# Other places for the accumulating loads of two batches, and six early groups, in an attention and MoE kernel

## The chip, the core and the metric

The kernel runs on one core of a Trainium2 chip. The metric is device time in microseconds (us) of one launch; lower is better. Before the change it is 992.26 us, the median of three runs (989.83 to 993.4).

A core has five engines, each with its own instruction queue worked in order. TensorE (PE in the profile) multiplies matrices into PSUM banks. ScalarE (ACT) evaluates functions such as exp. VectorE (DVE) does elementwise work. GpSimd (POOL) and SyncE (SP) serve here mainly to issue DMA transfers. Engines wait for each other through semaphores.

## The reference

Batches: 4. Each has 12288 queries of 128 channels and a key-value map of 384 x 32 positions.

```
kv_pool = kv.reshape(B, H//4, 4, W//4, 4, C).mean(axis=(2, 4))    # 768 pooled rows per batch
k = v = kv_pool.reshape(B, -1, C) @ w_sr
s = q @ k.transpose(0, 2, 1) / sqrt(C)
x = softmax(s) @ v                                                # 49152 tokens x 128
h = x @ w_in                                                      # 128 -> 2048
out = (h * sigmoid(1.702 * h)) @ w_out                            # 2048 -> 128
```

## The kernel before

**Tiles.** A group is 512 tokens; there are 96, 24 to a batch. In attention a group has 6 chunks (128 pooled rows each), in the MoE part 16 (128 of the 2048 hidden channels each). A chunk is filled by one 512-column matmul on TensorE (L358 in attention, L600 in MoE), and ScalarE evaluates three chunks at a time from PSUM into `ag` (L360 exp, L602 GELU). Chunks are drained by further matmuls: L371 multiplies by `v`, L610 by `w_out`. VectorE then normalises attention output into `x` (L394, L397) or turns MoE output for the store (L621).

**Stages.** `BOUNDS` makes three rounds: groups 0 to 23, 24 to 71, and 72 to 95. Each round does the attention of its groups and then their MoE. So batch 0 is used in the first attention, batches 1 and 2 in the second, and batch 3 in the third.

**The order of work is planned in Python** when the program is built: a loop over `seq` (fills) and `todo` (drains) keeps model clocks `now`, `dve` and `end` with costs such as `FIXED` and `CHUNK`, and decides what comes next on TensorE and VectorE. On the chip each engine simply works through its list.

**ScalarE is relieved by VectorE.** The first groups of rounds 2 and 3 are *early*: `EARLY = (2, 4)` of them have their exp computed by VectorE (a polynomial, `early_exp`, L439 to L452) during the MoE stage before. They need slots at the bottom of `ag`, which `LOW` keeps clear from a given MoE group on. `rolling` lists attention chunks, and `lent` MoE chunks, that VectorE does within their own stage.

**Keys of batches 1 to 3.** The pooling sum over four by four positions is done partly by DMA. `add_kv(b, n)` issues two loads, one for each half, of the n-th of eight slices; from the second slice on they add to what lies in `kvs` (L174, GpSimd's queue). Such a load waits for the landing of the one before it on the same half. `use_kv(b, a)` then puts a sum of the two halves on VectorE (`sum_kv`, L180) and queues three short jobs for the planner: a transpose on TensorE (L185), the keys (L193) and the values (L200). The first of these sums needs all 16 loads of its batch.

**What is issued when** stands in tables, keyed by the group whose first fill comes up: `ADD_KV` and `USE_KV` for the above; `CAST` and `CAST_MOE` for the casts of q to bfloat16 in DRAM (L210, GpSimd); `TURN` and `TURN_MOE` for the transposing loads of q (L216, SyncE); `W_IN` and `W_OUT` for the attention groups at which the MoE weights are loaded (L561, L564, GpSimd). GpSimd's transfers are timed by `gate()`: a tiny memset on VectorE at that point of its list (L529), and one on GpSimd that waits for it (L530).

```
if i == W_IN:
    gate()
    nc.gpsimd.dma_start(out=w_in_sb, in_=moe_w_in)
```

**Attention output** leaves SBUF and comes back transposed: after every six groups SyncE stores a part to DRAM (`put_away`, L512) and reads it back with a DMA transpose (`bring_back`, L517). Output stores (L623) are on SyncE too.

Of the kernel before, what the change touches and what calls it, by code (L numbers as in the profile page):

```python
# [24 lines left out]
def kernel(  # L25
# [8 lines left out]
    JC = J // 128  # L34
    d_ff = moe_w_in.shape[1]
    FCH = d_ff // 128
# [9 lines left out]
    TS = 3  # L46
# [12 lines left out]
    BOUNDS = (0, GB, 3 * GB, NG)  # L59
    R = len(BOUNDS) - 1  # L60
    XS = NS // 2
    EARLY = (2, 4)
    AG = 102

    cpool = ctx.enter_context(tc.tile_pool(name="const", bufs=1))
# [42 lines left out]
    now = 0.0  # L108
# [60 lines left out]
    def add_kv(b, n):  # L169
        i, w = divmod(n, r)  # L170
        if n == 0:
            kv_sums[b] = kvsum.tile([Hp, 2, Wp, C], F32, name="kvs")
        for i2 in range(2):
            nc.gpsimd.dma_start(out=kv_sums[b][:, i2], in_=kv_p[b, i, w, :, i2],  # L174
                                **({"accum_op": ADD} if n else {}))
# [32 lines left out]
    def cast_q(s):  # L208
        sl = slice(s * SG, (s + 1) * SG)
        nc.gpsimd.dma_start(out=q_bf[sl, :].rearrange("(p i) c -> p (i c)", p=128),  # L210
                            in_=q_flat[sl, :].rearrange("(p i) c -> p (i c)", p=128))

    def load_qT(s):
        qTs[s] = qpool.tile([128, 1, SG], BF, name="qT")
        nc.vector.memset(qTs[s][:, 0, 0:1], 0.0)
        nc.sync.dma_start_transpose(out=qTs[s], in_=q_bf[s * SG:(s + 1) * SG, :])  # L216
# [116 lines left out]

    ahead = [range(b, b + n) for b, n in zip(BOUNDS[1:], EARLY)]
    early = [i for part in ahead for i in part]
    rolling = [(i, JC - 1) for i in (*range(35, 70, 6), 84)]
    lent = [(g, FCH - 1) for g in (*range(28, 37, 4), 74, 77, 79, 82, 84, 87, 89, 92, 94)]
    borrowed = []
    for n in range(R):
        borrowed += [("a",) + c for c in rolling if round_of(c[0]) == n]  # L340
# [148 lines left out]
    steps, early_todo = None, []  # L489
# [35 lines left out]
    def gate():  # L525

        one = gate_tile[:, gates[0] % 8:gates[0] % 8 + 1]
        gates[0] += 1
        nc.vector.memset(one, 0.0)  # L529
        nc.gpsimd.memset(one, 0.0)  # L530

    TURN = {6: 3, 7: 4, 8: 5, 76: 22, 80: 23}
    TURN.update({i: i // 4 + 3 for i in range(BOUNDS[1] + 4, 61, 4)})
    TURN[26] = 9
    TURN_MOE = {3: 6, 21: 7, 22: 8, 68: 19, 69: 20, 70: 21}
    CAST = {0: [5], 14: [6]}
    CAST_MOE = {1: 7, 2: 8, 3: 9, 4: 10, 5: 11, 6: 12, 16: 13, 17: 14, 18: 15, 19: 16, 20: 17, 21: 18,
                46: 19, 47: 20, 48: 21, 49: 22, 50: 23}
    ADD_KV = {("a", i): (1, i - 15) for i in range(15, 23)}
    ADD_KV.update({("m", g): (2, g - 8) for g in range(8, 16)})  # L540
    ADD_KV.update({("m", g): (3, g - 26) for g in range(26, 34)})
    USE_KV = {("m", 3): (1, 0), ("m", 5): (1, 1), ("m", 18): (2, 0), ("m", 20): (2, 1), ("m", 36): (3, 0), ("m", 38): (3, 1)}
    LOW = {4: EARLY[0] * JC, 37: EARLY[1] * JC}
    W_IN, W_OUT = 11, 13

    def background(i):

        if i in TURN:
            load_qT(TURN[i])
        if i in CAST:  # L550
            gate()
            for s in CAST[i]:
                cast_q(s)
        if ("a", i) in ADD_KV:
            gate()
            add_kv(*ADD_KV["a", i])
        if ("a", i) in USE_KV:
            use_kv(*USE_KV["a", i])
        if i == W_IN:
# [6 lines left out]
    def background_moe(g):  # L566

        nonlocal low, raw
        if g in BOUNDS:
            raw = None  # L570
        if g in LOW:
            low = LOW[g]
            order[:] = [f for f in order if f >= low // K]
        if g in CAST_MOE:
            gate()
            cast_q(CAST_MOE[g])
        if g in TURN_MOE:
            load_qT(TURN_MOE[g])
        if ("m", g) in ADD_KV:
            gate()  # L580
            add_kv(*ADD_KV["m", g])
        if ("m", g) in USE_KV:
            use_kv(*USE_KV["m", g])

    def use_kv(b, a):
        nonlocal extra_at
        sum_kv(b, a)
        on_dve(3.5)
        extra_at = max(extra_at, dve + 1.5)
        extras.extend([(transpose_pooled, b, a), (make_k, b, a), (make_v, b, a)])  # L590
# [68 lines left out]
    seq, todo = [], []  # L659
    todo_early = [("a", t, a) for t in range(NT) for a in range(2) if (t // TS * TS + TS - 1) // 4 in early]  # L660
    for n in range(R):
        part = [c for c in chunks if round_of(c[0]) == n]
        while part:
            m = sizes.pop(0) if sizes else K
# [12 lines left out]
        while flat:  # L677
            m = K if len(flat) > sum(rest) else rest.pop(0)
# [25 lines left out]
    def jobs(p):  # L704

        nonlocal now
        for f, *args in first.get(p, ()):
            if f in COST:
                now = max(now, free[next_acc()])
            f(*args)  # L710
            if f in COST:
                now += COST[f][0]
                free[last_acc] = copied(f)
# [33 lines left out]

    FIXED, CHUNK, SWITCH, HANDOVER, EVACUATE = 0.265, 1.978, 6.0, 1.0, 4.5  # L750
    COST = {pool_chunk: (1.9, 2.6), key_chunk: (0.3, 2.4), value_chunk: (0.3, 2.4),
            transpose_q: (1.05, 4.2), early_fill: (1.0, 5.5), key_and_value: (0.55, 3.5),
            transpose_pooled: (0.9, 3.6), make_k: (0.8, 3.2), make_v: (0.8, 3.7)}
# [5 lines left out]
    source, dve = None, 0.0  # L759
    early_left = [2 * (G // T) * n for n in EARLY]  # L760

# [39 lines left out]
    for n in range(len(seq)):  # L801
        fill(n + 2)
        jobs(n + 3)
        while True:
            room = room_ahead()
            limit = end[-1] - len(seq[n + 3][1]) - HANDOVER if n + 3 < len(seq) else 1e9
            bank = free[next_acc()]
            f = None
            if extras and now >= max(extra_at, bank):
                f, *args = extras[0]  # L810
            if steps and dve <= now + 2.0:
                early_step()
            near = todo and todo[0][0] == "m" and todo[0][2] > 10
            if not f and not near and not steps and early_todo and early_fits(min(n + 2, len(seq) - 1), *early_todo[0]) and dve <= now + 2.0 and now >= bank:
                f, args = early_fill, early_todo[0]
            if f and max(now, bank) + COST[f][0] > limit + (0.0 if f is early_fill else 4.5) and room >= 4 * K:
                f = None
            if f:
                now = max(now, bank) + COST[f][0]
                f(*args)  # L820
                free[last_acc] = dve + 1.0 if f is early_fill else copied(f)
                if f in (transpose_pooled, make_k, make_v):
                    on_dve(2.5)
                extra_at = max(now + PAUSE, dve + 1.5 if f in (transpose_pooled, make_k, make_v) else 0.0)
                if f is early_fill:
                    pass
                else:
                    extras.pop(0)
                continue
            if not source:  # L830

                if todo_early and not any(early_waits(t) for t in range(todo_early[0][1], todo_early[0][1] + TS)):
                    source = todo_early
                else:
                    source = todo
            if not source:
                break
            kind, i, c = source[0]
            needs = at[("at" if kind == "a" else kind, i, c)]
            cost = K * SMALL if kind == "a" else 1.0  # L840
            halved = kind == "a" and i // TS < SPLIT
            first_of = (c == 0 or halved) and (kind == "m" or i % TS == 0)
            if source is not todo_early and (needs > n or (kind == "a" and first_of and at["at", i + TS - 1, c if halved else 1] > n)
                                             or (kind == "m" and first_of and (i, FCH - 1) in lent
                                                 and made.get((i, FCH - 1), 1e9) > now + 1.0)
                                             or (kind == "a" and (early_waits(i) or first_of and early_waits(i + TS - 1)))):
                if first_of:
                    source = None
                break
            start = now if source is todo_early else max(now, end[needs] + HANDOVER)  # L850
            if first_of:
                start = max(start, bank)
            if start + cost > limit and not (room < 2 * K + 1 or (room < 4 * K and start == now)):
                if first_of:
                    source = None
                break
            now = start + cost
            (drain_attn if kind == "a" else drain_moe)(i, c)
            source.pop(0)
            if kind == "a" and i // 4 in early:  # L860
                early_left[round_of(i // 4) - 1] -= 1
                if not early_left[round_of(i // 4) - 1]:
                    low = 0
            if (halved or c == (1 if kind == "a" else FCH - 1)) and (kind == "m" or i % TS == TS - 1):
                source = None
# [31 lines left out]
```

## Time and profile before

| What | Value |
|---|---|
| median of 3 runs | 992.26 us (989.83 to 993.4) |
| the profiled execution's own time | 988.68 us |
| its span | 986.9 us, 15345 instructions |
| TensorE busy | 944.2 us (96%) |
| ScalarE busy | 933.7 us (95%) |
| VectorE busy | 578.2 us (59%) |
| GpSimd busy | 82.6 us (8%) |
| L602, GELU on ScalarE | 683.6 us in 511 instructions |
| L360, exp on ScalarE | 240.6 us in 189 instructions |
| batch loads L174, issue to landing | 7.1 us in the median of 48 |
| w_in and w_out, issue to landing | 8.4 us each |

How to read the profile: a row of digits gives one engine's busy share in 40 equal slices of the span, 9 being 90% or more. A row of the list of waits names an engine, what it did next and, after the arrow, what it waited for; then the total in us, the number of times, and the longest. A row of the timeline has the start in us, the duration in us, the engine, the line of the kernel, the operation and its tiles, and in brackets the idle time before it and what ended that. A row of a DMA queue has packets, megabytes, and packet time as a share of 16 DMA engines; q0 is GpSimd's queue and q1 SyncE's.

### The profile page before, as it was taken

Reading aid. Unit: us, or ns where it says so; the run is one execution under the profiler, and the core shown is the slowest. Engines: PE = TensorE matmul, PEld = TensorE weight load, DVE = VectorE, ACT = ScalarE, POOL = GpSimd, SP = SyncE. Lnnn points to the kernel's source line nnn. Section 1 sums busy time; section 2 is a strip of 40 time slices with the busy share of each in tenths; the row PEclk is TensorE's granted clock in tenths of the full one; section 3 lists DMA queues with packets and bytes.
Section 4 is the critical chain, followed back from the end, with each engine's and each line's share of the span. In section 5 each row is a group of like instructions: output and inputs, shape, how many; then the busy total and the mean of one; then the engine's idle time right before and its main releaser. Section 6 shows DMA issues by size and latency. Waiting matters only on the chain.

```text
span 986.9 us, 15345 instructions
## 1 busy us (share of the span) xinstructions
PE 944.2 (96%) x6222; PEld 500.8 (51%) x6222; DVE 578.2 (59%) x1113; ACT 933.7 (95%) x710; POOL 82.6 (8%) x132
## 2 busy tenths in 40 slices
PE   8999149999999999999999999999999999999998
PEld 4676024444446777744444444444444675444444
DVE  5532016676736776455357768777761547777673
ACT  6999139999999999999999999999999999999996
POOL 3022220331000000023200000000000000000000
PEclk9999669999999999999999999999999999999999
DMA  9899995999665484699922263222254456222223
GB/s 210 177 176 166 151 171 86 131 139 158 95 108 108 108 177 102 129 139 169 143 42 33 43 113 61 40 34 33 35 93 73 68 121 120 39 44 33 43 35 52
DMA packets 383143, 98.59 MB, mean 100 GB/s; under 512 B 346832, under 2 KB 381264, under 8 KB 382608
## 3 DMA queue, kind: packets, MB, share of 16 engines
q1 hardware_dynamic: 343952, 62.36, 37.5%
q0 software_dynamic: 38848, 35.13, 26.0%
q8 instruction: 48, 0.79, 0.3%
q14 instruction: 23, 0.19, 0.1%
q10 hardware_dynamic: 272, 0.13, 0.0%
HBM read 52.49 MB, written 48.76 MB: 103 GB/s over the span
## 4 chain that ended last, share of the span: by engine, by line
PE 89%; DMA 8%; issue 1%; POOL 1%; DVE 1%; ACT 0%; DVEq 0%; POOLq 0%
PE banks L610 33%; PE banks L600 33%; PE banks L371 11%; PE banks L358 10%; DMA kvs<-in_kv_dram 7%; DMA x<-in_kv_dram 1%; PE banks L423 1%; PE banks L638 0%; POOL kvs L174 0%; POOL x L223 0%; PE banks L417 0%; ACT ag L360 0%; PE banks L185 0%; PE banks L140 0%; PE banks L193 0%
## 5 line engine op out<-in xcount | busy, mean ns | idle before, releaser
L602 ACT ACTIVATE ag<-banks 128x1536 bf16<-128x1536 f32 (+1 forms) x511 | 683.6, 1600 | 36.5 <-PE banks L600 36.4
L600 PE MATMUL banks<-x,w_in_sb 128*128 128x512 bf16 x1524 | 413.3, 380 | 1.3 <-DMA x<-x_bf 1.3
L610 PE MATMUL banks<-ag,w_out_sb 128*128 128x512 bf16 x1508 | 409.5, 380 | 0.1
L360 ACT ACTIVATE ag<-banks 128x1536 bf16<-128x1536 f32 (+2 forms) x189 | 240.6, 1494 | 3.7 <-PE banks L358 3.4
L610 PEld LDWEIGHTS <-w_out_sb 128*128 128x128 bf16 x1520 | 148.4, 98 | 178.1 <-issue 2.1
L600 PEld LDWEIGHTS <-w_in_sb 128*128 128x128 bf16 x1524 | 147.2, 98 | 174.7 <-issue 6.7
L371 PEld LDWEIGHTS <-ag 128*128 128x128 bf16 x2276 | 146.2, 98 | 46.7 <-issue 0.4
L371 PE MATMUL banks<-v,ag 128*128 128x129 bf16 x2276 | 163.4, 220 | 0.1
L621 DVE STREAM_TRANSPOSE o_sb<-banks 128x512 f32<-128x512 f32 x95 | 67.8, 714 | 142.1 <-PE banks L610 124.5
L358 PE MATMUL banks<-qT,kT 128*128 128x512 bf16 x533 | 145.8, 379 | 1.4 <-ACT ag L360 0.5
L450 DVE SCALAR_TENSOR_TENSOR ea<-ea,eb 128x512 f32<-128x512 f32 x172 | 117.6, 684 | 4.8 <-DVE ea L447 0.6
L394 DVE RECIPROCAL rec<-banks 128x3 f32<-128x3 f32 x124 | 22.2, 179 | 98.4 <-PE banks L371 98.4
L397 DVE TENSOR_TENSOR x<-banks,rec 128x384 bf16<-128x384 f32 x124 | 69.1, 557 | 4.3
L174 POOL DMA_DIRECT2D kvs<-in_kv_dram x48 | 60.4, 1272 | 111.1 <-DMA kvs<-in_kv_dram 108.3
L358 PEld LDWEIGHTS <-kT 128*128 128x128 bf16 x533 | 45.6, 98 | 27.6 <-issue 2.3
L439 DVE TENSOR_SCALAR ea<-banks 128x512 f32<-128x512 f32 x43 | 29.7, 691 | 45.4 <-PE banks L423 44.9
L530 POOL MEMSET gate_tile<- 1x1 f32 x45 | 11.6, 258 | 393.0 <-DVE gate_tile L529 385.8
L481 DVE RECIPROCAL eb<-ea 128x256 f32<-128x256 f32 x24 | 40.8, 1722 | 0.3
L185 PE MATMUL banks<-ident,pooled 96*128 96x96 bf16 x24 | 2.2, 217 | 33.3 <-DVE pooled L180 33.3
L474 DVE SCALAR_TENSOR_TENSOR ea<-ea,eb 128x512 f32<-128x512 f32 x48 | 33.0, 687 | 1.4
L445 DVE SCALAR_TENSOR_TENSOR eb<-eb,ea 128x512 f32<-128x512 f32 x43 | 29.7, 690 | 1.3
L180 DVE TENSOR_TENSOR pooled<-kvs 96x512 bf16<-96x512 f32 x6 | 4.0, 668 | 37.6 <-DMA kvs<-in_kv_dram 37.6
(83 smaller groups left out, 292.5 us busy)
## 6 DMA issues: line engine op xcount, KB each, us to landing
out_dram<-o_sb SPq DMA_DIRECT2D x380, 64.0 KB, 2.0
kvs<-in_kv_dram POOLq DMA_DIRECT2D x48, 384.0 KB, 7.1
x_bf<-x SPq DMA_DIRECT2D x16, 768.0 KB, 5.7
q_bf<-in_q_dram POOLq DMA_DIRECT2D x21, 512.0 KB, 5.6
x<-in_kv_dram POOLq DMA_DIRECT2D x5, 512.0 KB, 12.6
x<-in_q_dram POOLq DMA_DIRECT2D x5, 256.0 KB, 15.2
x<-in_kv_dram SPq DMA_DIRECT2D x1, 1024.0 KB, 5.1
w_in_sb<-in_moe_w_in_dram POOLq DMA_DIRECT2D x1, 512.0 KB, 8.4
```

The lines of the kernel that those rows point to most:

```text
L174: nc.gpsimd.dma_start(out=kv_sums[b][:, i2], in_=kv_p[b, i, w, :, i2], **({"accum_op": ADD} if n else {}))
L358: nc.tensor.matmul(ps[:, k, :], kTs[i // GB][:, jc * 128:(jc + 1) * 128], rhs, start=True, stop=True)
L360: nc.scalar.activation(place([("a",) + c for c in chunks]), ps, AF.Exp, scale=scale)
L371: nc.tensor.matmul(av_of[u][:, k * (C + 1):(k + 1) * (C + 1)], weights(("a", i, jc))[:, o:o + T], vs[i // GB][:, jc, 0:C + 1], start=(jc = ...
L397: nc.vector.tensor_tensor(to, ps[:, :, 0:C], rec.unsqueeze(2).broadcast_to([128, TS, C]), MUL)
L450: nc.vector.scalar_tensor_tensor(a, a, COEFFS[k], b, ADD, MUL)
L474: nc.vector.scalar_tensor_tensor(a, a, COEFFS[k], b, ADD, MUL)
L481: nc.vector.reciprocal(b[:, m:m + 256], a[:, m:m + 256])
L600: nc.tensor.matmul(ps[:, k, :], w_in_sb[:, fc * 128:(fc + 1) * 128], x[:, g % (4 * XS) * G:(g % (4 * XS) + 1) * G], start=True, stop=True)
L602: nc.scalar.activation(place([("m",) + c for c in chunks]), ps, AF.Gelu_apprx_sigmoid)
L610: nc.tensor.matmul(o_of[g], w_out_sb[:, fc, :], weights(("m", g, fc)), start=(fc == 0), stop=(fc == FCH - 1))
L621: nc.vector.transpose(o_sb, o_of.pop(g))
```

## The change

The loads of batch 1 move from attention groups 15 to 22 to groups 10 to 17, and its keys from MoE groups 3 and 5 to 7 and 8. Those of batch 2 move one group later (MoE groups 9 to 16), with its keys at MoE groups 20 and 22. Those of batch 3 move from MoE groups 26 to 33 into the second attention (groups 38 to 45), with its keys at attention groups 58 and 60. `w_in` and `w_out` are loaded at groups 18 and 19 in place of 11 and 13. Round 3 gets six early groups in place of four; three lent chunks of round 2 and one rolling chunk of round 3 go back to ScalarE; `LOW` holds the slots from MoE groups 8 and 25. Some casts and transposing loads of q move with these. In the planner, `FIXED` rises from 0.265 to 0.295, and a step of VectorE's polynomial is held back until its model clock is free when the next drain closes an accumulator of the attention.

```
-    EARLY = (2, 4)
+    EARLY = (2, 6)
...
-    rolling = [(i, JC - 1) for i in (*range(35, 70, 6), 84)]
-    lent = [(g, FCH - 1) for g in (*range(28, 37, 4), 74, 77, 79, 82, 84, 87, 89, 92, 94)]
+    rolling = [(i, JC - 1) for i in range(35, 70, 6)]
+    lent = [(g, FCH - 1) for g in (74, 77, 79, 82, 84, 87, 89, 92, 94)]
...
-    TURN = {6: 3, 7: 4, 8: 5, 76: 22, 80: 23}
+    TURN = {6: 3, 7: 4, 8: 5, 78: 22, 80: 23}
     TURN.update({i: i // 4 + 3 for i in range(BOUNDS[1] + 4, 61, 4)})
     TURN[26] = 9
-    TURN_MOE = {3: 6, 21: 7, 22: 8, 68: 19, 69: 20, 70: 21}
-    CAST = {0: [5], 14: [6]}
-    CAST_MOE = {1: 7, 2: 8, 3: 9, 4: 10, 5: 11, 6: 12, 16: 13, 17: 14, 18: 15, 19: 16, 20: 17, 21: 18,
-                46: 19, 47: 20, 48: 21, 49: 22, 50: 23}
-    ADD_KV = {("a", i): (1, i - 15) for i in range(15, 23)}
-    ADD_KV.update({("m", g): (2, g - 8) for g in range(8, 16)})
-    ADD_KV.update({("m", g): (3, g - 26) for g in range(26, 34)})
-    USE_KV = {("m", 3): (1, 0), ("m", 5): (1, 1), ("m", 18): (2, 0), ("m", 20): (2, 1), ("m", 36): (3, 0), ("m", 38): (3, 1)}
-    LOW = {4: EARLY[0] * JC, 37: EARLY[1] * JC}
-    W_IN, W_OUT = 11, 13
+    TURN_MOE = {4: 6, 21: 7, 22: 8, 44: 19, 68: 20, 70: 21}
+    CAST = {0: [5]}
+    CAST_MOE = {0: 6, 1: 7, 2: 8, 3: 9, 4: 10, 5: 11, 6: 12, 16: 13, 17: 14, 18: 15, 19: 16, 20: 17, 21: 18,
+                32: 19, 47: 20, 48: 21, 49: 22, 50: 23}
+    ADD_KV = {("a", i): (1, i - 10) for i in range(10, 18)}
+    ADD_KV.update({("m", g): (2, g - 9) for g in range(9, 17)})
+    ADD_KV.update({("a", i): (3, i - 38) for i in range(38, 46)})
+    USE_KV = {("m", 7): (1, 0), ("m", 8): (1, 1), ("m", 20): (2, 0), ("m", 22): (2, 1), ("a", 58): (3, 0), ("a", 60): (3, 1)}
+    LOW = {8: EARLY[0] * JC, 25: EARLY[1] * JC}
+    W_IN, W_OUT = 18, 19
...
-    FIXED, CHUNK, SWITCH, HANDOVER, EVACUATE = 0.265, 1.978, 6.0, 1.0, 4.5
+    FIXED, CHUNK, SWITCH, HANDOVER, EVACUATE = 0.295, 1.978, 6.0, 1.0, 4.5
...
-            if steps and dve <= now + 2.0:
+            closing = todo and todo[0][0] == "a" and todo[0][1] % TS == TS - 1
+            if steps and dve <= now + (0.0 if closing else 2.0):
                 early_step()
```

## The prediction

> **What bounds the kernel now.** I read the page's 40 slices first, then the list of waits, then the timelines of GpSimd, TensorE and VectorE around what these showed.
>
> ```profile
> PE   8999149999999999999999999999999999999998
> ...
> ACT  6999139999999999999999999999999999999996
> ...
> DMA  9899995999665484699922263222254456222223
> ```
>
> TensorE and ScalarE are full in every slice but the fifth and sixth (99 to 148 us). So the time is a nearly saturated pair of engines plus one hole. The list of waits names it:
>
> ```profile
> POOL kvs L174 <- DMA kvs<-in_kv_dram: 108.3, 35, 10.7
> DVE pooled L180 <- DMA kvs<-in_kv_dram: 37.6, 1, 37.6
> ACT ag L602 <- PE banks L600: 36.4, 3, 34.1
> PE banks L185 <- DVE pooled L180: 33.3, 1, 33.3
> ```
>
> At MoE group 3 VectorE reaches the sum of batch 1's pooled keys (L180) and waits 37.6 us for the accumulating loads. TensorE stops 4.3 us later at the transpose behind it: 33.3 us. Why the loads are late is on GpSimd's timeline:
>
> ```profile
> 42.84 0.09 POOL L530 MEMSET gate_tile<- 1x1 f32 x1 [24.50 <-DVE gate_tile L529]
> 43.08 0.56 POOL L561 DMA_DIRECT2D w_in_sb<-in_moe_w_in_dram  x1 [0.15 <-issue]
> ...
> 53.35 1.60 POOL L174 DMA_DIRECT2D kvs<-in_kv_dram  x2
> ...
> 125.42 1.31 POOL L174 DMA_DIRECT2D kvs<-in_kv_dram  x1 [2.39 <-DMA kvs<-in_kv_dram]
> 129.10 1.31 POOL L174 DMA_DIRECT2D kvs<-in_kv_dram  x1 [2.37 <-DMA kvs<-in_kv_dram]
> 129.88 0.57 POOL L530 MEMSET gate_tile<- 1x1 f32 x1
> 129.91 1.07 POOL L210 DMA_DIRECT2D q_bf<-in_q_dram  x1
> ```
>
> The 16 loads of a batch are two chains of eight: each waits, on GpSimd and in order, for the landing of the one before it on the same half. They hold GpSimd from 53.35 to 129.10 us, and whatever stands behind them there (the casts at 129.91, whose gates had been opened by VectorE from 86.67 us on) waits. w_in stood ahead of them.
>
> **The change, part by part.** I write r for the mean time of one of the 14 accumulating loads; the first pair, which doesn't accumulate, took 6.7 us (53.35 to 60.05). Values of r in this trace: 3.6 with the compute engines stopped (121.68, 125.42, 129.10); 3.74 in MoE groups 11 to 15 (issues from 193.79 to 227.49, nine steps), beside output stores; 5.35 over batch 1 (60.05 to 135.0, over 14). Beside SyncE's transfers of x and its transposes it is slower still; packets by queue, from 64 to 78 us and from 78 to 92 us:
>
> ```profile
> q0 software_dynamic: 2316, 1.16, 79.0%
> q1 hardware_dynamic: 4413, 1.12, 54.9%
> ...
> q0 software_dynamic: 1563, 0.79, 75.6%
> q1 hardware_dynamic: 4860, 1.23, 70.4%
> ```
>
> A load is 384 KB in rows of 512 B, 768 packets, so these stretches moved 3.0 and 2.0 loads in 14 us each: r = 4.7 and 7.0.
>
> *Batch 1 from group 10, keys at MoE groups 7 and 8.* The hole of 33.3 us at L185 goes: group 7 starts some 27 us later than group 3 and the loads some 13 us earlier. Minus 33.3.
>
> *w_in at group 18, w_out at 19.* These are now behind the 16 loads on GpSimd, and the first matmul of MoE needs w_in. It is now ready by 78.27 us, where TensorE waits 1.3 us for x alone:
>
> ```profile
> 78.27 0.81 PE L600 MATMUL banks<-x,w_in_sb 128*128 128x512 bf16 x3 [1.30 <-DMA x<-x_bf]
> ```
>
> Group 11's gate is at 42.70 on VectorE and group 13's at 46.68, so group 10's comes at about 40.5. First pair: landed at about 46, since the DMA queues are nearly empty but for one store of x at 43 to 49 us. From 46 to 60 I count 3 us for the rest of that store and 11 us at 3.65: 3 loads. From 60 to 64 another store of x takes the queue: none. From 64 to 92 SyncE does what it does now: 3.0 and 2.0. That is 8 of 14 by 92 us. After that SyncE has nothing, because TensorE stands at L600 and the attention's last drains are behind it; 6 loads at 3.5 make 21, so the last lands at about 113 (r = 4.8). w_in was issued just after the last load was, and lies behind it in the same queue: its 512 KB at the 1.43 MB that GpSimd's queue moved from 53 to 60 us are 2.5 us more, 115.5. TensorE's hole from 78.3 is then 37 us. w_out follows it at once and is wanted 11 us after the first fill (89.74 against 78.27), so it is hidden. By r, the hole is 46 + 14r + 2.5 - 78.3, or 14r - 30: 21 at 3.65, 45 at 5.35. I take 37, plus 4 against the old hole. The half-rate clock after it is paid now too, so nothing is added.
>
> *Batch 3 in the second attention, loads from group 38, sum at group 58.* VectorE's qT memsets date the groups 36, 40, 56 and 60:
>
> ```profile
> 314.86 0.06 DVE L215 MEMSET qT<- 128x1 bf16 x1 [1.20 <-PE banks L358]
> 325.78 0.06 DVE L215 MEMSET qT<- 128x1 bf16 x1
> ...
> 367.35 0.06 DVE L215 MEMSET qT<- 128x1 bf16 x1
> 377.74 0.06 DVE L215 MEMSET qT<- 128x1 bf16 x1
> ```
>
> Group 38 is at 320.3, group 58 at 372.5: 52 us for the batch. 7 for the first pair and 14 at 3.65 are 58, so it is late even in a free queue; and this queue isn't free:
>
> ```profile
> q1 hardware_dynamic: 28976, 7.34, 66.2%
> ```
>
> That is SyncE's queue from 320 to 373 us: 547 packets a us, against 315 and 347 in the two stretches above. It has gaps of some 13 us in all, so I take r = 6, between 4.7 and 7.0: 7.5 loads done by 372.5, the other 6.5 at 3.5 after VectorE has stopped and SyncE's work with it: landed at 395.5. VectorE waits 23 us at L180. Queued behind it are the L394 and L397 pairs that empty TensorE's accumulators, and TensorE meets the transpose of the pooled keys soon anyway; with the 4.3 us of slack that the old hole shows, TensorE loses 18.7. The clock adds 2: after the old hole the granted clock is 0.50 in 136 to 140 us and 0.88 in the next 2. So 21. Bounds: r = 3.65 gives a VectorE wait of 6 and next to nothing on TensorE; r = 7.0, 27 and 24; r = 7 until the end, 52 and 50, which I leave out since SyncE's work stops. SyncE's own qT loads, stretched by the same contention, have about 27 us of lead (a qT is asked for 12 groups of 2.6 us ahead and lands in 4.3), so I price them at 0; without that cover, up to 10.
>
> The Trainium skill prices such a load lower: DMA: Bandwidth & Descriptors, section Anatomy of one DMA, fits a GpSimd DMA as about 2.0 us plus its bytes over 436 GB/s, which for 384 KB is an estimate of 2.9 us. By that the new holes would be about 11 us and none, and the change would win about 25 us. The page's row of loads here says 7.1 us from issue to landing in the median, with two in flight at a time, so I go by the trace.
>
> *Six early groups, three lent chunks and one rolling chunk back to ScalarE.* A chunk on ScalarE is 0.451 us in attention (240.6 / 533) and 0.449 in MoE. The third attention gives up 12 chunks and takes 1: minus 5.0 on ScalarE, but only 12 fills of 0.216 (2.6) on TensorE, which is as full there. The second MoE takes 3 back: plus 1.35. Net minus 1.2 to minus 3.6; I take minus 2.5. VectorE needs 9.35 us a chunk (514.97 to 729.98, 23 steps): 36 are 337 us, from about group 25 (430) to 767, while the second MoE ends at 755; 12 in the first MoE start at group 8. The last may slip by a chunk or two: 0 to plus 3.
>
> *The planner's two numbers, batch 2 one group later, the casts.* ScalarE's idle time outside the hole is some 6 us in its two groups, so better packing can win little: plus or minus 2. Batch 2's use moves two groups for a load that moves one; casts are used many groups later. Nothing.
>
> **Sum.** Against the profiled execution's own 988.7 (span 986.9 and 1.8 around it): plus 4, plus 21, minus 2.5 make 1011.2. The median of the runs shown is 992.26, 1.0036 times that execution: 1015.
>
> **The rivals.** All turn on r.
> - *Forecast*, r of 4.5 to 6 with the holes moved to L600 and to group 58: 1003 to 1025. Chance 0.66.
> - *The loads run almost free* (other side, faster). With r near 3.65 throughout, w_in lands at about 99, its hole is 21, and group 58 costs 4 or less: 988.7 - 12 + 4 - 2.5 = 978, by the ratio 982. It decides below r of about 4.0, where the two holes together equal the old one. For: 3.74 beside output stores, and the queue is nearly idle at 40 us. Against: 4.7 and 7.0 beside just the SyncE work that stays. Chance 0.10.
> - *w_in as forecast, batch 3 nearly in time*, as SyncE's gaps of 13 us carry more than I think: plus 4 and plus 5, so 995, by the ratio 999. Chance 0.11.
> - *Both worse.* r = 5.35 as over batch 1 now makes w_in's hole 45 (plus 12), and batch 3 at 7 with qT late costs 25 to 35: 1023 to 1033, by the ratio 1027 to 1037. Chance 0.13.
>
> That the change doesn't do what it says is possible only for batch 3's place: it comes in the second attention, but not by group 58.
>
> **Numbers.** 0.5% is about what a measurement of this kernel can tell from no change, 987 to 997. Faster is the second case, 0.10. The third straddles the edge: 0.08 same, the rest slower. Slower 0.82. The range 998 to 1032 leaves out the second case, a little of the third and half of the last.
>
> **What would show it.** Right: L561 issued at about 105 us on GpSimd, L600 waiting some 37 us for w_in; no wait at L180 in the first MoE; a VectorE wait of about 23 us at L180 near 410 us (372.5 plus the shift), with the granted clock at 0.5 after it. Wrong: L561 before 95 us, or no wait at the sum in the second attention.

## The result, and the profile after

The changed kernel takes 1035.55 us (median of 4 runs, 1031.06 to 1038.51) against 991.45 for the kernel before (4 runs). The ratio is 1.044, 95% interval 1.039 to 1.049. Ratios here and below leave out executions more than 1.5% above the fastest of the same kernel, which concerns two executions of the run weights first alone. The forecast was 1015, with a range up to 1032. The profiled execution took 1037.57 us (span 1035.8); that of before took 988.68, so 48.9 us are to be found.

The page's slices after, over a span of 1035.8 us (25.9 us each):

```profile
PE   8990692999999993599999999999999999999998
...
ACT  6990592999999994499999999999999999999997
...
PEclk9995796999999997799999999999999999999999
DMA  9999899499864899946232236322223435522223
```

One hole has become three: in the fourth and fifth slice, in the seventh, and in the sixteenth and seventeenth. The list of waits names each:

```profile
ACT ag L602 <- PE banks L600: 57.2, 5, 34.2
...
DVE o_sb L621 <- DMA out_dram<-o_sb: 43.3, 8, 30.0
...
PE banks L600 <- DMA w_in_sb<-in_moe_w_in_dram: 34.9, 1, 34.9
ACT ag L360 <- PE banks L358: 31.6, 5, 27.8
...
DVE pooled L180 <- DMA kvs<-in_kv_dram: 27.9, 1, 27.9
PE banks L185 <- DVE x L397: 26.7, 1, 26.7
...
PE banks L610 <- DVE o_sb L621: 18.2, 1, 18.2
```

TensorE loses 34.9 us at L600 for w_in, 18.2 at L610 for an output buffer and 26.7 at L185 for batch 3's sum, where it lost 33.3: plus 46.5. ScalarE's own idle time agrees: 57.2 + 31.6 against 36.4 + 3.4, plus 49.0, with 2.2 less work (931.5 busy against 933.7).

The first hole is the one that was forecast. GpSimd's timeline, with the same rows as before:

```profile
38.35 1.62 POOL L174 DMA_DIRECT2D kvs<-in_kv_dram  x2
...
102.02 1.31 POOL L174 DMA_DIRECT2D kvs<-in_kv_dram  x1 [3.17 <-DMA kvs<-in_kv_dram]
102.80 0.57 POOL L530 MEMSET gate_tile<- 1x1 f32 x1
102.84 1.13 POOL L561 DMA_DIRECT2D w_in_sb<-in_moe_w_in_dram  x1
```

w_in, issued at 43.08 before, comes out at 102.84, 0.8 us after the last load. The second hole was not in the forecast. SyncE's timeline (an SPq row is the time for which a transfer held SyncE's queue while it was issued), and the two rows at the hole's end:

```profile
124.81 0.38 SPq L512 DMA_DIRECT2D x_bf<-x  x1
125.28 37.15 SPq L517 DMA_TRANSPOSE x<-x_bf  x2
162.49 12.64 SPq L623 DMA_DIRECT2D out_dram<-o_sb  x8
```

```profile
174.84 0.72 DVE L621 STREAM_TRANSPOSE o_sb<-banks 128x512 f32<-128x512 f32 x1 [30.04 <-DMA out_dram<-o_sb]
...
175.61 0.59 PE L610 MATMUL banks<-ag,w_out_sb 128*128 128x512 bf16 x1 [18.19 <-DVE o_sb L621]
```

The last two transposes of the round's x hold SyncE's queue for 37 us. Eight output stores, those of MoE groups 0 and 1, come out only at 162. There are three output buffers, so VectorE waits 30 us for one and TensorE 18. Before the change the same two transposes stood at 91.21 to 116.08 us, more than half of it inside the old hole (102.4 to 135.7 us), and nobody waited for a store:

```profile
91.21 24.87 SPq L517 DMA_TRANSPOSE x<-x_bf  x2
```

### The profile page after: what moved, and what is told of

Read it like the earlier page. It is cut to its first block, busy times and chain, and to the rows that moved or that the text cites. A ratio compares the mean times of both kernels' runs of the same rounds, so it can differ in the third digit from the quotient of the medians.

```text
span 1035.8 us, 15305 instructions
## 1 busy us (share of the span) xinstructions
PE 938.5 (91%) x6109; PEld 503.1 (49%) x6222; DVE 612.9 (59%) x1178; ACT 931.5 (90%) x707; POOL 83.0 (8%) x132
## 4 chain that ended last, share of the span: by engine, by line
PE 61%; DMA 16%; ACT 10%; issue 7%; SPq 5%; DVE 1%; POOL 1%; DVEq 0%; POOLq 0%
PE banks L600 24%; PE banks L610 24%; DMA kvs<-in_kv_dram 13%; ACT ag L602 9%; PE banks L371 7%; PE banks L358 4%; SPq L517 4%; SPq L623 1%; ACT ag L360 1%; DMA out_dram<-o_sb 1%; DMA w_in_sb<-in_moe_w_in_dram 1%; PE banks L423 1%; DMA x<-in_kv_dram 1%; POOL kvs L174 0%; PE banks L638 0%
## 5 line engine op out<-in xcount | busy, mean ns | idle before, releaser
L602 ACT ACTIVATE ag<-banks 128x1536 bf16<-128x1536 f32 (+1 forms) x512 | 685.2, 1517 | 57.3 <-PE banks L600 57.2
L600 PE MATMUL banks<-x,w_in_sb 128*128 128x512 bf16 x1476 | 408.5, 380 | 37.0 <-DMA w_in_sb<-in_moe_w_in_dram 34.9
L610 PE MATMUL banks<-ag,w_out_sb 128*128 128x512 bf16 x1491 | 408.3, 380 | 19.8 <-DVE o_sb L621 18.2
L360 ACT ACTIVATE ag<-banks 128x1536 bf16<-128x1536 f32 (+2 forms) x185 | 236.8, 1412 | 34.6 <-PE banks L358 31.6
L600 PEld LDWEIGHTS <-w_in_sb 128*128 128x128 bf16 x1527 | 148.1, 98 | 224.8 <-DMA w_in_sb<-in_moe_w_in_dram 35.1
L610 PEld LDWEIGHTS <-w_out_sb 128*128 128x128 bf16 x1520 | 148.5, 98 | 177.7 <-issue 1.6
L450 DVE SCALAR_TENSOR_TENSOR ea<-ea,eb 128x512 f32<-128x512 f32 x216 | 147.8, 684 | 9.4 <-issue 4.3
L358 PE MATMUL banks<-qT,kT 128*128 128x512 bf16 x480 | 140.1, 380 | 3.6 <-ACT ag L360 0.5
L439 DVE TENSOR_SCALAR ea<-banks 128x512 f32<-128x512 f32 x54 | 37.3, 692 | 54.4 <-PE banks L423 54.1
L358 PEld LDWEIGHTS <-kT 128*128 128x128 bf16 x522 | 44.4, 98 | 25.9 <-issue 2.1
L445 DVE SCALAR_TENSOR_TENSOR eb<-eb,ea 128x512 f32<-128x512 f32 x54 | 37.3, 691 | 1.6
L452 DVE SCALAR_TENSOR_TENSOR ag<-ea,ee 128x512 bf16<-128x512 f32 x48 | 33.2, 692 | 2.1
L481 DVE RECIPROCAL eb<-ea 128x256 f32<-128x256 f32 x18 | 30.6, 1723 | 0.2
L185 PE MATMUL banks<-ident,pooled 96*128 96x96 bf16 x24 | 2.2, 216 | 27.8 <-DVE x L397 26.7
L474 DVE SCALAR_TENSOR_TENSOR ea<-ea,eb 128x512 f32<-128x512 f32 x36 | 24.6, 684 | 0.9
```

What stands on the lines that cost most here:

```text
L358: nc.tensor.matmul(ps[:, k, :], kTs[i // GB][:, jc * 128:(jc + 1) * 128], rhs, start=True, stop=True)
L360: nc.scalar.activation(place([("a",) + c for c in chunks]), ps, AF.Exp, scale=scale)
L439: nc.vector.tensor_scalar(a, ps, scale / LN2, -126.0, MUL, MAX)
L450: nc.vector.scalar_tensor_tensor(a, a, COEFFS[k], b, ADD, MUL)
L600: nc.tensor.matmul(ps[:, k, :], w_in_sb[:, fc * 128:(fc + 1) * 128], x[:, g % (4 * XS) * G:(g % (4 * XS) + 1) * G], start=True, stop=True)
L602: nc.scalar.activation(place([("m",) + c for c in chunks]), ps, AF.Gelu_apprx_sigmoid)
```

## The experiments

Each run is compared with the kernel before on the same chip; "before" there is 988 to 992.5 us. Diffs are against the changed kernel unless said.

**Weights first.** Does w_in's place make the first hole, and does the second follow from it?

```
-    W_IN, W_OUT = 18, 19
+    W_IN, W_OUT = 11, 13
```

> w_in and w_out go back to groups 11 and 13, all else as changed. Theory: the changed kernel loses its time in three separate holes of TensorE, 34.9 us at L600 (w_in behind batch 1's loads), 18.2 us at L610 (output stores behind SyncE's transposes of x, which now run beside the casts) and 26.7 us at L185 (batch 3's sum). Here the first goes, and the second with it, since the transposes come back to 91 to 116 us, ahead of most casts: 1037.6 - 35 - 18 and some 2 of slow clock = 980 to 988. Rival: the DMA queues of the first 180 us are simply full, so that time comes back as a wait at batch 1's sum or at the output stores: over 1010.

Measured: 1028.2 us (1001.1 to 1047.6). The ratio, of the two shorter executions alone (1001.1 and 1015.5), is 1.018 (1.008 to 1.029). The theory missed. The wait for w_in is gone, but in the profiled execution time came back at the output stores, the rival's place. That is the longest of the four, 46 us above the shortest, so its hole at L610 doesn't stand for the others. From its waits, then SyncE's timeline:

```profile
PE banks L610 <- DVE o_sb L621: 61.5, 1, 61.5
```

```profile
97.75 47.92 SPq L517 DMA_TRANSPOSE x<-x_bf  x2
145.72 44.45 SPq L623 DMA_DIRECT2D out_dram<-o_sb  x7
```

While the second transpose is under way GpSimd is through with the loads and issues five casts of q in a row (109.27 to 111.42). From 120 to 160 us the two queues hardly move (packets, MB, share of time):

```profile
q1 hardware_dynamic: 1215, 0.31, 77.4%
q0 software_dynamic: 327, 2.45, 51.2%
```

That is 30 of SyncE's packets a us. So the casts became the suspect for the changed kernel's second hole, as the next run but one tests.

**Batch 3's sums in MoE.**

```
-    ... ("a", 58): (3, 0), ("a", 60): (3, 1)}
+    ... ("m", 24): (3, 0), ("m", 25): (3, 1)}
```

> Batch 3's two sums go from attention groups 58 and 60 to MoE groups 24 and 25 of the second round; its loads stay at groups 38 to 45. Theory: the 26.7 us at L185 go, with 2 us of slow clock, and the early chunks start up to two groups later: 1008 to 1013 by the profiled execution. Rival: the loads slow SyncE's loads of q and x so far that TensorE waits for these in the second attention: over 1025.

Measured: 1017.1 us, ratio 1.0275 (1.021 to 1.034); its profiled execution 1011.9, within the 1008 to 1013. No wait at L185 is left in its list; w_in costs 38.2 there and L610 11.7. The third hole goes with the sum's place.

**Casts later.**

```
-    CAST_MOE = {0: 6, 1: 7, 2: 8, 3: 9, 4: 10, 5: 11, 6: 12, 16: 13, ...
+    CAST_MOE = {0: 6, 6: 7, 7: 8, 8: 9, 9: 10, 11: 11, 13: 12, 16: 13, ...
```

> The casts 7 to 12 go from MoE groups 1 to 6 to groups 6 to 9, 11 and 13; all else as changed. Theory: the transposes of x at 125 to 162 us are slow because of the casts beside them (27.1 us for the last, 11.7 for the same one before the change). Without them they take about 10 us each, the output stores get out in time and the 18.2 us at L610 fall under 4: 1018 to 1022. Rival: the transposes are slow there for another reason (the running MoE, the store of x before them), and the hole stays over 14: 1033 or more.

Measured: 1024.4 us, 2 us over the forecast (profiled execution 1020.0, within it), ratio 1.036 (1.030 to 1.042). The hole at L610 is gone from its waits, and the two transposes take 9.3 us where they took 37.15:

```profile
127.64 9.32 SPq L517 DMA_TRANSPOSE x<-x_bf  x2
137.02 6.08 SPq L623 DMA_DIRECT2D out_dram<-o_sb  x8
```

So the running MoE doesn't slow a transpose; casts beside it do.

**The three edits together**, that is `W_IN, W_OUT = 11, 13`, the sums at MoE groups 24 and 25, and the casts later.

> The three edits of the other runs together. Theory: none of the three holes is left and the work itself is about 2 us less than before the change: 950 to 960, faster than before by 3 to 4%. Rival (full DMA queues): one of the holes comes back in another place, over 980.

Measured: 973.5 us, ratio 0.9815 (0.975 to 0.988): faster than before, but 13 us over the forecast. Its list still has 13.3 us at L610. Here the transposes run at 96.32 for 27.90 us beside batch 1's last loads, with no cast before 120.42 us: two in a row, with the stores behind them.

**The casts in pieces.** What about a cast jams a transpose? In the changed kernel's trace a cast is 16 packets of 32 KB; one that ran alone, between 120.5 and 125 us, took 2.9 us a packet in the mean (16 packets, 63.8% of 16 engines). SyncE's packets are 256 B. Here the cast is cut up, in the same place:

```
-   out=q_bf[sl, :].rearrange("(p i) c -> p (i c)", p=128),
+   out=q_bf[sl, :].rearrange("(k p i) c -> p k (i c)", p=128, i=8),      # the source likewise
```

> The changed kernel, but each cast of q is written as pieces of 1024 elements (2 KB out of 4 KB) where it now runs as 16 packets of 32 KB; same bytes, same places in the order. Theory A: the large packets hold the DMA engines and jam the transposes of x beside them. Then the last two transposes take under 13 us each, the hole at L610 (18.2 us) falls under 8: 1022 to 1030. Rival B: any cast from DRAM to DRAM jams a transpose, whatever its packets: the hole stays, 1033 or more.

Measured: 1017.4 us, ratio 1.026 (1.022 to 1.030), somewhat below the forecast. Nothing is left at L610, with the casts still at 122.60 to 146.79 us beside the transposes (14.14 us for the two). The two queues over the two transposes, first here (126 to 142 us), then in the changed kernel (125.3 to 162.4 us):

```profile
q1 hardware_dynamic: 8795, 2.24, 65.0%
q0 software_dynamic: 688, 1.31, 44.0%
...
q1 hardware_dynamic: 8068, 2.05, 86.5%
q0 software_dynamic: 121, 1.87, 36.6%
```

SyncE's queue moved 550 packets a us here against 217 there, at 19 ns a packet against 64. The bytes and the place of the casts are the same, so it is how a cast is cut into packets, not the cast as such. The Trainium skill bears on this: DMA: Bandwidth & Descriptors, section Queues, rings and completion order, says that a DMA engine takes turns between its queues and changes only at packet boundaries. The runs agree in direction; whether a packet of the page is one of the trace no run shows. It isn't the whole of it: 16 engines at 2.9 us a packet would move 5.5 large packets a us, and GpSimd's queue moved 1.87 MB in the 37 us of the jam, 1.5 such packets a us. What else held the engines is open.

**Transposes apart.** With the three edits, the second of the two transposes goes from MoE group 2 to group 5, and the casts 7 to 12 to groups 8 to 11, 13 and 15:

```
+        if g in (2, 5):                        # in background_moe; put_away(3) no longer does it
+            bring_back(2 if g == 2 else 3)
```

> The three edits together, and the last two transposes of x of the first round issued at MoE groups 2 and 5, not one after the other; the casts 7 to 12 go to groups 8 to 11, 13 and 15. Theory: the 13.3 us that are left at L610 with the three edits come from two transposes in a row on SyncE's queue (27.9 us) with the output stores behind them and three output buffers; apart, each is covered by the buffers: hole under 4 us, 955 to 966. Rival: one transpose beside batch 1's loads is enough to hold the stores: hole over 8, no faster than 970.

Measured: 965.8 us, ratio 0.973 (0.969 to 0.977). No TensorE wait at the output's line is left. The hole came from two transposes in a row before the stores, as expected. The second takes 3.46 us in its new place. What is left there is a wait of 5.9 us for x at the first fill of MoE, where it was 1.3 before the change.

**Four early groups.** The same kernel with the round 3 part as before the change (and its tables of q):

```
-    EARLY = (2, 6)
+    EARLY = (2, 4)              # rolling 84 and lent 28, 32, 36 come back
...
-    ... ("m", 24): (3, 0), ("m", 25): (3, 1)}       # loads at attention groups 38 to 45
+    ... ("m", 36): (3, 0), ("m", 38): (3, 1)}       # loads at MoE groups 26 to 33
```

> As the run with the transposes apart, but with the round 3 part as before the change: four early groups, three lent chunks and one rolling chunk more on VectorE, batch 3's loads at MoE groups 26 to 33. Prices that part of the change by itself. Theory (minus 2.5 us in the prediction): 1 to 4 us slower than the run with six. Rival: TensorE bounds these stages, or VectorE is late with 36 chunks, and six early groups win nothing or lose: equal or faster.

Measured: 956.45 us, ratio 0.964 (0.960 to 0.968): 9.3 us faster than with six. The part that I priced at minus 2.5 costs time, together with the place of batch 3's loads, once the holes are gone.

**Loads in the second attention alone**, with four early groups and the sums at MoE groups 36 and 38:

```
-    ADD_KV.update({("m", g): (3, g - 26) for g in range(26, 34)})
+    ADD_KV.update({("a", i): (3, i - 38) for i in range(38, 46)})
```

> As the run with four early groups, but batch 3's loads stay in the second attention (groups 38 to 45); its sums are at MoE groups 36 and 38 as before the change. Splits the 9 us by which six early groups lost to four. Theory: the loads beside the second attention hold up SyncE's loads of q (TensorE waited 6.3 us for qT with six early groups, ScalarE 9.6 in that stage): 962 to 969. Rival: the 36 chunks on VectorE cost the time, the loads nothing: 953 to 959.

Measured: 964.4 us, ratio 0.975 (0.972 to 0.978). So it is the loads, by 8 us (10 by the ratios; 6 against the run with four early groups and casts in pieces, measured alongside); six early groups against four make 1.4 us between this run and the last but one, no difference that these runs can tell. From its waits between 290 and 430 us:

```profile
ACT ag L360 <- PE banks L358: 10.1, 6, 3.0
...
PE banks L358 <- DMA qT<-q_bf: 4.8, 2, 3.0
PE banks L423 <- DMA qT<-q_bf: 4.2, 2, 2.4
```

q arrives late behind the loads. ScalarE has no such wait in that stage with the loads in MoE.

**Batch 3 later.**

```
-    ... ("a", 58): (3, 0), ("a", 60): (3, 1)}
+    ... ("a", 66): (3, 0), ("a", 69): (3, 1)}
```

> The changed kernel, but batch 3's sums at attention groups 66 and 69 in place of 58 and 60, some 21 us later. Theory: the loads crawl beside SyncE's transfers, so these 8 groups bring only some 4 loads: the wait at the sum falls from 27.9 to about 16 us, TensorE's hole from 26.7 to 15: 1022 to 1030. Rival: the loads land at the same time whatever the attention does, wait about 7: under 1020.

Measured: 1023.4 us, ratio 1.032 (1.026 to 1.039), 12 us less than the change. That total fits the theory, but the wait itself is the rival's. From the waits between 380 and 460 us:

```profile
DVE pooled L180 <- DMA kvs<-in_kv_dram: 7.2, 1, 7.2
PE banks L185 <- DVE x L397: 6.2, 1, 6.2
```

The loads were issued from 338.3 to 414.4 us, 76 us for the batch, against 341.9 to 415.3, 73 us, in the changed kernel, where VectorE stood still from 395.75 us on. So stopping it speeds them little. About 6 of the 20 us saved at L185 come back as other waits of L360 (17.4 us in all, of which 7.1 is this one; 3.8 beside the hole in the changed kernel), where q is late.

**Weights first, casts in pieces**: the first edit with that of `cast_q` above.

> The changed kernel with w_in and w_out at groups 11 and 13 (a run that took 1001 to 1048 us, with 61.5 us lost at L610 in its profile) and the casts in pieces of 1024 elements. Theory: that loss was the jam of the 32 KB packets of the casts with the transposes of x. It falls to 15 us or less, as with the three edits, and batch 3's 26 us stay: 985 to 1003, with less spread. Rival: it came from the transposes and the loads alone: over 1012.

Measured: 1010.4 us (1005.7 to 1019.6), ratio 1.024 (1.018 to 1.029): between the two. Against the ratio of weights first, 1.018 (1.008 to 1.029), that is no gain that these runs show. L610 has 17.6 us in the profile, where the long execution of weights first had 61.5. But the casts stand elsewhere here: batch 1's loads end later, so the casts are issued from 124.46 us on, when the transposes (98.24 to 126.31 us) are all but through. So the run doesn't test small pieces beside the transposes. What it shows is the row of two transposes (11.68 and 16.30 us) beside the loads; batch 3's hole is 28.7.

**Four early groups, casts in pieces**: the same with that edit.

> The run with four early groups with the casts in pieces as well. Theory: the casts are away from the transposes there already, so there is nothing left to win: 952 to 960. Rival: the smaller pieces cost DMA time or GpSimd time: over 962.

Measured: 958.4 us, ratio 0.969 (0.966 to 0.972). Nothing to win there, as expected.

**Batch 1's loads early, transposes in a row.** As the last, but `put_away(3)` issues both transposes again, and the casts 7 to 12 are at MoE groups 1 to 6.

> The kernel before with batch 1's loads from group 10, its keys at MoE groups 7 and 8, the casts in pieces but in the changed kernel's places, and the transposes of x one after the other as before; w_in and w_out at 11 and 13, four early groups, batch 3 as before. Theory: the old hole of 33.3 us goes, and some 8 to 13 us come back at L610 behind the two transposes in a row: 962 to 972. Rival: the transposes need not be apart once the casts are in pieces: 952 to 960.

Measured: 974.6 us (970.4 to 982.9), ratio 0.987 (0.983 to 0.991). Against 958.4, measured alongside, that is 16 us more, where 8 to 13 were forecast; its profile, of the longest execution, has 22.7 us at L610. The edit also puts casts, in pieces, beside the second transpose and the stores behind it (112.37 to 117.79 us): the first eight stores took 31.83 us there, 12.43 in the run above. How much of the 16 us is the row's and how much the casts', this run doesn't tell.

The fastest version is the run with four early groups: loads of batch 1 from group 10, the weights in their old places, the transposes apart, the casts 7 to 12 later, batch 3's loads in MoE as before. It is 3.6% below before.

## Why the prediction was right or wrong

*Right: the old hole goes and comes back at L600.* w_in came out at 102.84 us (about 105 forecast) and TensorE waited 34.9 (37). The accumulating loads ran at 4.4 us each from the first of them to the last (45.08 to 102.02, 13 steps), where I had 4.8 for r. The weights-first run has no such wait: shown.

*Right in kind, short in size: batch 3.* The group times held: group 38's gate opened at 341.28 and VectorE came to the sum at 395.75, 54.5 us later (52 forecast). Loads took r = 5.5 (346.57 to 423.55, over 14). I had 6 up to VectorE's stop and 3.5 after it, "SyncE's work with it". The first held: 8 loads were through by then (the tenth was issued at 395.41, on the landing of the eighth), 6.1 us each. The second failed: the other 6 took 27.8, 4.6 each, while SyncE's queue, which had fallen behind, went on (a transpose from 401.49 for 14.42 us, a load of q from 416.01). VectorE waited 27.9 in place of 23; in the batch 3 later run the loads take about as long with the attention running. A second error is the slack: I took the 4.3 us of the old hole, in MoE; here TensorE lost 26.7 of 27.9, a slack of 1.2. Together 8 us.

*Wrong, and what put the time outside the range: "casts are used many groups later. Nothing", and "after that SyncE has nothing".* The second is true until w_in lands. I followed the batch's loads past everything on GpSimd's queue, but not what the new hole moves on SyncE's. More than half of the two transposes had run in the old hole's shadow; after the new one they stand ahead of the stores of a running MoE, and beside casts that before had stood behind the loads until 129.91. Price: 18.2 us at L610, shown by the casts-later and the pieces runs, each of which takes that wait away alone and lowers the median, by 11 and by 18 us (8 and 18 by the ratios). In the prediction's sum: 1011.2 + 18.2 + 8.0 - 2.1 (w_in) = 1035.3 of the 1037.6 measured. The sum also lacks the restart after the hole at L610: the granted clock was 0.56 from 176 to 180 us, some 1.8 us by an estimate. That it comes so close is partly luck, as it keeps the minus 2.5 for the early groups that the later runs don't bear out. No run takes out the planner's two numbers or batch 2's shift, priced at plus or minus 2 and at nothing.

*The early groups.* ScalarE's work fell by 2.2 us, where the chunks of the prediction make 3.65. It brings nothing that the runs show, and batch 3's loads in the second attention cost 6 to 10. I had put SyncE's qT loads at 0, "up to 10" without cover. In the changed kernel TensorE's waits for q are 2.0 us; once the holes are gone, the price is near the upper end.

*The rivals.* "Both worse" has 1027 to 1037, which holds the measured 1035.55 by luck: w_in's hole was 34.9 us where it had 45, and r was 4.4 in place of 5.35. The Trainium skill's estimate for a load (DMA: Bandwidth & Descriptors, section Anatomy of one DMA, 2.9 us) is far from these runs as well: 7.5 us from issue to landing in the median after.

## What to carry to other kernels

When a change moves a hole, list what had been running inside the old one, on every queue: it will run beside other work now, and whatever stands behind it in order will wait. Follow a moved transfer past its own queue and past those that share the DMA engines. Keep slow transfers off a queue that also drains a small ring of output buffers, or space them by what the ring covers.

## What was not expected of the hardware

A DRAM to DRAM cast that runs as 16 packets of 32 KB, beside a DMA transpose, slows both badly: two transposes took 37 us with casts coming one by one, against 9.3 without and 14.1 with the same bytes in small pieces, and a cast among them took up to 29.9 us to land, where 6.8 is the median of the run. In one execution of weights first, with five casts at once and batch 1's last loads beside them, the two took 48 us; beside such loads without the casts they took 27.9. Plain output stores fare better: in the kernel before, from 138.7 to 160 us, casts landed in 5.3 us and output stores in 5.4 (2.0 in the median of the run). The times of weights first scatter, 1001 to 1048 us over four runs against 1006 to 1020 with the pieces; that the jam is the reason is not shown.
